# Value tiles padded by the host to full width, and value rows loaded one chunk ahead, in a chunked recurrence followed by a mixture of experts

## The chip, the core and the metric

One core of a Trainium2 chip runs the whole program. The metric is the time of one execution in device microseconds (us), the median of several runs. Engines are named as the profile names them: PE (TensorE), DVE (VectorE), ACT (ScalarE), POOL (GpSimd) and SP (SyncE, which here issues nearly all transfers).

## What is computed

The first stage is a recurrence over 768 time steps for 4 batches of 8 heads, with a 40x40 state per head. The second stage is a mixture of 8 experts over the 3072 x 320 result, with weights P from a gate that a Sinkhorn iteration balances.

```python
for t in range(S):
    y[:, :, t] = einsum('bhd,bhde->bhe', rt, state)
    Sa = einsum('bhde,bhe->bhd', state, at)
    state = state * wt[:, :, None, :] - einsum('bhd,bhe->bhde', Sa, bt) + einsum('bhd,bhe->bhde', vt, kt)
...
for e in range(E):
    out += P[:, e:e + 1] * (np.maximum(x @ w1[e], 0.0) @ w2[e])
```

All data are 32-bit floats. `v` holds the value rows of the recurrence (`vt` in the code above, one vector of 40 per head and step).

## The kernel before, in words

The recurrence is cut into 12 chunks of 64 steps (`C`, `NCH`). A unit of work is one chunk `c` of one batch `b`: eight heads, as four pairs (`NP`). The two heads of a pair stand on partitions 0 to 39 and 64 to 103 of tiles with 104 partitions (`R2`), and unused partitions hold zeros.

Work that doesn't depend on the state is done ahead by `prep(c, b)`. It loads one packed tile `inp` (L109, w, k, b and a of the unit), makes decay products by scans on DVE (`q` L114, `g` L122), the scaled `kb` and `ab` on DVE or POOL (L133, L139, L140), the products `ll` and the transposes `kt` on PE (L145, L153), and stores a part `lt` to DRAM as `ld`. For every two chunks, triangular matrices from `ld` are inverted on DVE (L170 to L182, tiles `un`, `lu`, `pr`). The inverse goes through DRAM (`ud`, `nd`) into `td` and `tt` (`tload`, `tmat`).

The sequential part is `recur(c, b)`, 48 units. It is a generator with five steps. The first step issues three loads on SP: the value rows into the left 64 columns of each pair's part of the tile `vz` (L238), `rb` (L240), and the transposed values into columns 64 to 103 of each head's part of the tile `f` (L242). Then PE makes `av` from `vz` and `rb` (L251), and DVE masks it into the left 64 columns of `f` (L252). The following steps are `xc` (L259), `pu` (L270, which needs `tt`), `c` and `ws` (L277, L279), the outputs `y` (L281, stored to DRAM as `xd` by L285) and the new state `z` (L292). At the end the transposed state is copied by ACT into columns 64 to 103 of the next `vz` (L299, L300). That `vz` is taken from five buffers (`vz_b`) in rotation. At the program's start all five are cleared once on DVE (`clear`, L85), since the loads leave a part of them unwritten. `f` has three buffers and `rb` two. A store `lp` of gate products is fed in between (L307, L312).

The units of the four batches are interleaved: step k of unit (c, b) has the due time 5c + k + 1.1b, the preps, inversions and loads have due times of their own, and the events are emitted sorted by them. Within each engine a scheduler then places the instructions by its own simulation of the program. An engine runs its list strictly in order, so a waiting instruction holds up everything behind it, on SP too. Transfers issued on SP tell of their landing through eight counters, `DMAHW0` to `DMAHW7`, used in turn.

The second stage reads `xd` back as `xs` (L508, L510), splits it and the expert weights `ws` (L473) into high and low parts, and multiplies on PE (`p` L545, `op` L610). It starts while the last recurrence units run.

Of the kernel before, what the change touches and what calls it, by code (L numbers as in the profile page):

```python
# [17 lines left out]
NB, NH, S, D = 4, 8, 768, 40  # L18
C = 64
NCH = S // C  # L20
NP = 4
R2 = 104
# [6 lines left out]
def attention(ctx, tc, d, xd, ps, pq, pt, gs, lg):  # L29
    nc = tc.nc  # L30
# [35 lines left out]
    lg_b = [const.tile([128, 4 * NP, 64], F32, name="lg")]  # L66
    ab_b = [pin.tile([R2, NP, 128], F32, name=f"ab{i}") for i in range(2)]
    g1_b = [pin.tile([R2, NP, 64], F32, name=f"g1{i}") for i in range(1)]
    vz_b = [const.tile([R2, NP, 104], F32, name=f"vz{i}") for i in range(5)]
    c1_b = [const.tile([R2, NP, 104], F32, name=f"c1{i}") for i in range(2)]  # L70
# [10 lines left out]
    def clear():  # L81
        nc.gpsimd.memset(unf, 0.0)
        nc.gpsimd.memset(unf[:, 0:1024:33], 1.0)
        for t in vz_b + c1_b + lg_b:
            nc.vector.memset(t, 0.0)  # L85
        for t in tt_b:
            nc.gpsimd.memset(t, 0.0)
# [11 lines left out]
    def rot(key, lst):  # L99
        i = state[key]  # L100
        state[key] = (i + 1) % len(lst)
        return lst[i]
# [132 lines left out]
    def recur(c, b):  # L235
        pp = preps[c, b]
        vz, zc = vz_cur[b], zp[b]
        nc.sync.dma_start(out=vz[:, :, 0:64], in_=d["v"][c, b])  # L238
        rb = io.tile([R2, NP, 128], F32, name="rb", bufs=NRB)
        nc.sync.dma_start(out=rb, in_=d["r"][c, b])  # L240
        f = wk.tile([R2, NP, 2, 104], F32, name="f", bufs=NFB)
        nc.sync.dma_start(out=f[0:64].rearrange("s p h x -> s (p h) x")[:, :, 64:104],  # L242
                          in_=d["vt"][c, b].rearrange("s (g x) -> s g x", x=40))
        if zc is None:
            nc.gpsimd.memset(f[64:104].rearrange("s p h x -> s (p h) x")[:, :, 64:104], 0.0)
        else:
# [3 lines left out]
        for p in range(NP):  # L250
            nc.tensor.matmul(av[:, p], lhsT=vz[:, p], rhs=rb[:, p], start=True, stop=True)  # L251
        nc.vector.tensor_tensor(  # L252
            out=f[:, :, :, 0:64], in0=av,
# [30 lines left out]
        for h in range(2):  # L284
            nc.sync.dma_start(  # L285
                out=xd[h * 160:h * 160 + 160].rearrange("(p e) t -> e p t", e=40)[:, :, tok:tok + 64],
                in_=y[h * 64:h * 64 + 40])
# [7 lines left out]
        zt = ps.tile([40, NP, 104], F32, name="zt", tag="ps")  # L295
        for p in range(NP):
            nc.tensor.transpose(zt[:, p], z[:, p], ident[0:R2, 0:R2])
        vz = rot("vz", vz_b)
        nc.scalar.copy(out=vz[0:40, :, 64:104], in_=zt[:, :, 0:40])  # L299
        nc.scalar.copy(out=vz[64:104, :, 64:104], in_=zt[:, :, 64:104])  # L300
        zp[b] = z
# [19 lines left out]

    gq, gcount = deque(), [0]
    vz_cur = [rot("vz", vz_b) for _ in range(NB)]
    preps, invs, tts = {}, {}, {}

    def start_seg(s):
# [9 lines left out]
    def load_lu(s, n):  # L336
        ld = invs[s][0]
        for cc in range(n):
            for blk in range(2):
                for h in range(2):  # L340
# [3 lines left out]
                        in_=ld[cc, r0:r0 + 32].rearrange("j b p h s -> (b p) j h s")[:, :, h, r0:r0 + 32])  # L344

    ev = [(T_CLEAR, clear, ())]
    gens = {}
    def step(c, b):
        if (c, b) not in gens:
            gens[c, b] = recur(c, b)  # L350
        next(gens[c, b], None)
# [6 lines left out]
    for c in range(NCH):  # L358
# [3 lines left out]
        t = 5 * c + 2 - T_LEAD  # L362
# [3 lines left out]
    for s, cs in enumerate(GROUPS):  # L366
# [3 lines left out]
        for i in range(n):  # L370
            cb = (cs[0] + i // NB, i % NB)
            j = cb[0] * NB + cb[1] - NSX
            t = 5 * (j // 4) + 3 + SKEW * (j % 4) + 0.01
            t = max(t, t0 + P0 + PD * i) if s else -20 + 0.01 * i
# [54 lines left out]
def body(ctx, tc, d, out):  # L429
# [12 lines left out]
    with ExitStack() as actx:  # L442
        ps, pq, pt = (actx.enter_context(tc.tile_pool(name=f"a_ps{i}", bufs=n, space=bass.MemoryType.PSUM))
                      for i, n in enumerate((PC, PQ, PT)))
        nc.sync.dma_start(out=gs, in_=d["gate"])
        attention(actx, tc, d, xd, ps, pq, pt, gs, lg)
        nc.gpsimd.memset(ones, 1.0)
        nc.sync.dma_start(out=ident, in_=d["cst"][:, 232:360])
# [290 lines left out]
def _layout(inputs):  # L739
    g = {k: np.asarray(v, dtype=np.float32) for k, v in inputs.items()}  # L740

    def split(a):
        return a.reshape(NB, NP, 2, NCH, C, D).transpose(3, 0, 2, 5, 1, 4)

    def packed(a, fill=0.0):
        x = split(a)
        o = np.full((NCH, NB, R2, NP, C), fill, np.float32)
        o[:, :, 0:40] = x[:, :, 0]
        o[:, :, 64:104] = x[:, :, 1]
        return o  # L750

    w = packed(g["w"], 1.0)
    wr = np.zeros((NCH, NB, R2, NP, 65), np.float32)
    wr[..., 1:] = w[..., ::-1]
    wf = np.zeros((NCH, NB, R2, NP, 64), np.float32)
    wf[..., 1:] = w[..., :-1]
    wcat = np.concatenate([wr.reshape(NCH, NB, R2, 260), wf.reshape(NCH, NB, R2, 256)], -1)
    kb = np.stack([packed(g["k"]), packed(g["b"])], axis=4)
    inp = np.concatenate([wcat, kb.reshape(NCH, NB, R2, 512), packed(g["a"]).reshape(NCH, NB, R2, 256)], -1)
    x = split(g["r"])  # L760
    rb = np.zeros((NCH, NB, R2, NP, 2, C), np.float32)
    rb[:, :, 0:40, :, 0] = x[:, :, 0]
    rb[:, :, 64:104, :, 1] = x[:, :, 1]
    vt = g["v"].reshape(NB, NH, NCH, C, D).transpose(2, 0, 3, 1, 4).reshape(NCH, NB, C, NH * D)
    rows = [(2 * p + h) * D + e for h in range(2) for p in range(NP) for e in range(D)]
    w1 = g["moe_w1"].reshape(E, DM, FP, 2, 128)[:, rows].reshape(E, 2, 160, FP, 2, 128)
    w1 = w1.transpose(0, 3, 4, 1, 2, 5)
    wp = np.zeros((E, FP, 2, 2, 2, 128, 128), np.float32)
    wp[:, :, :, :, 0] = w1[:, :, :, :, 0:128]
    for i in range(3):  # L770
        wp[:, :, :, :, 1, 32 * i:32 * i + 32] = w1[:, :, :, :, 128:160]
    wp = wp.transpose(0, 1, 5, 2, 3, 4, 6).reshape(E, FP, 128, 2, 2, 256)
    w2 = g["moe_w2"].reshape(E, FP, 2, 128, DM).transpose(0, 1, 3, 2, 4).reshape(E, FP, 128, 2 * DM)
    wts = np.concatenate([wp[..., 1, 0, :], w2, wp[..., 0, 0, :], wp[..., 0, 1, :], wp[..., 1, 1, :]], -1)
    wg = g["moe_w_gate"].reshape(NP, 2, D, E).transpose(1, 2, 0, 3)
    gate = np.zeros((R2, NP, E), np.float32)
    gate[0:40], gate[64:104] = wg[0], wg[1]
    cst = np.zeros((128, 660), np.float32)
    i = np.arange(64)
    up = (i[:, None] < i[None, :]).astype(np.float32)  # L780
    cst[0:64, 0:64] = up
    cst[0:64, 64:128] = up
    cst[64:128, 64:128] = 1.0
    cst[0:64, 128:192] = up
    cst[64:128, 128:192] = up
    cst[:, 192:232] = 1.0
    cst[:, 232:360] = np.eye(128)
    cst[64:104, 360:400] = np.eye(40)
    cst[:, 400::65] = 1.0
    arrays = dict(inp=inp, r=rb.reshape(NCH, NB, R2, NP, 128), v=packed(g["v"]),  # L790
                  vt=vt, wts=wts, gate=gate, cst=cst)
    return {k: np.ascontiguousarray(v) for k, v in arrays.items()}

# [16 lines left out]
```

## Time and profile before

| what | value |
|---|---|
| median of 3 runs | 1891.57 us (1887.94 to 1893.3) |
| the profiled execution's own time | 1888.5 us |
| its span on the core | 1886.7 us |
| PE busy over the span | 1768.5 us (94%) |
| DVE busy over the span | 1395.1 us (74%) |
| first `pu` (needs the first inverse) | about 119 us |
| last `av` of the recurrence | 547.66 us |
| PE busy from 680 to 1887 us | 1202.71 of 1207 us |

The profiled execution's own time is 3.1 us below the median of the runs and lies between their ends. The span is counted from the first instruction. Rows of the profile with a time at their start are instructions or merged groups, in us from the start of the span, followed by their duration; a bracket holds the engine's idle time before it and what ended that. "SPq" is SP issuing or waiting. In the rows on stretches, each engine's busy time stands in turn, then the granted clock of PE as a share of full speed, the share of busy time of the 16 DMA engines, and GB/s.

### The profile page before, as it was taken

To read this page: it belongs to the slowest core of one execution; us is meant where nothing else is said; L and a number is where in the kernel's file an instruction comes from. 1 tells how busy PE (TensorE), PEld (TensorE's weight loads), DVE (VectorE), ACT (ScalarE), POOL (GpSimd) and SP (SyncE) were. 2 spreads that over 40 slices of the span, in tenths; PEclk is the share of its full clock that TensorE was granted. 3 is DMA by queue.
4 is the path that set the end of the run, shared out by engine and by line. 5 is a ranking of instruction groups with operands and counts; after the bars stand their busy time and mean duration, and the time that the engine had idled before them with its cause. 6 is when DMAs were issued, how large, how long until landed. Compare 5 with 4: busy or idle time off the path is not lost.

```text
span 1886.7 us, 31821 instructions
## 1 busy us (share of the span) xinstructions
PE 1768.5 (94%) x12035; PEld 1731.1 (92%) x12035; DVE 1395.1 (74%) x2330; ACT 853.9 (45%) x1845; POOL 896.9 (48%) x845
## 2 busy tenths in 40 slices
PE   4478989889998999999999999999999999999999
PEld 4368878789888999999999999999999999999999
DVE  7766768686579877776867777886776767777676
ACT  6346566655553444343433434345343433434342
POOL 6636457562345355371835628004461826537170
PEclk9568889988889999999999999999999999999999
DMA  8567777855732011110201102111110201111011
GB/s 192 102 131 160 137 156 144 176 128 102 164 96 70 32 43 37 37 61 14 73 26 49 55 19 74 55 33 38 37 55 19 73 19 56 37 37 57 17 37 42
DMA packets 187838, 136.26 MB, mean 72 GB/s; under 512 B 155941, under 2 KB 165285, under 8 KB 187685
## 3 DMA queue, kind: packets, MB, share of 16 engines
q1 hardware_dynamic: 184485, 128.98, 27.6%
q10 hardware_dynamic: 3200, 5.25, 1.1%
q8 instruction: 95, 1.56, 0.3%
q14 instruction: 58, 0.48, 0.1%
HBM read 113.74 MB, written 20.45 MB: 71 GB/s over the span
## 4 chain that ended last, share of the span: by engine, by line
PE 76%; DVE 10%; DMA 6%; issue 3%; POOL 2%; ACT 2%; SPq 1%; DVEq 0%; POOLq 0%; ACTq 0%
PE op L610 35%; PE p L545 32%; DMA inp<-in_inp_dram 2%; PE xc L259 2%; DVE pr L179 2%; PE pu L270 1%; PE av L251 1%; PE c L277 1%; DVE q L114 1%; PE ll L145 1%; PE lp L307 1%; PE gp L226 1%; DMA nd<-pr 1%; POOL ab L140 1%; DVE g L122 1%
## 5 line engine op out<-in xcount | busy, mean ns | idle before, releaser
L545 PE MATMUL p<-xch,wh 128*128 128x384 f32 (+1 forms) x1792 | 605.3, 339 | 5.2 <-DVE cs L654 1.8
L566 ACT ACTIVATE hh<-sm 128x384 fp32r<-128x384 f32 x512 | 269.5, 527 | 726.3 <-DVE sm L563 726.3
L610 PE MATMUL op<-wh,hh 128*128 128x320 f32 x1536 | 477.3, 311 | 1.0 <-ACT hh L566 0.9
L610 PE MATMUL op<-wl,hh 128*128 128x320 f32 x1536 | 474.7, 310 | 0.0
L610 PE MATMUL op<-wh,hl 128*128 128x320 f32 x1536 | 468.0, 310 | 4.4 <-DVE hl L569 4.4
L491 POOL TENSOR_TENSOR wl<-ws,wh 128x640 fp32r<-128x640 f32 x60 | 103.1, 1719 | 608.4 <-ACT wh L489 608.1
L569 DVE SCALAR_TENSOR_TENSOR hl<-sm,hh 128x384 fp32r<-128x384 f32 x512 | 370.8, 757 | 2.8 <-ACT hh L566 2.3
L545 PEld LDWEIGHTS p<-xch,wh 128*128 128x128 f32 (+1 forms) x1792 | 337.9, 189 | 8.4 <-DVE u L563 2.7
L545 PE MATMUL p<-xcl,wh 128*128 128x384 f32 x896 | 303.1, 338 | 0.0
L545 PE MATMUL p<-xch,wl 128*128 128x384 f32 x896 | 302.3, 337 | 0.0
L610 PEld LDWEIGHTS op<-wh,hh 128*128 128x128 f32 x1536 | 290.6, 189 | 1.7 <-ACT hh L566 1.5
L610 PEld LDWEIGHTS op<-wh,hl 128*128 128x128 f32 x1536 | 287.1, 188 | 5.4 <-DVE hl L569 5.3
L610 PEld LDWEIGHTS op<-wl,hh 128*128 128x128 f32 x1536 | 291.4, 190 | 0.0
L563 DVE TENSOR_TENSOR sm<-p,u 128x384 f32<-128x384 f32 x384 | 232.6, 615 | 9.2 <-PE p L545 0.4
L545 PEld LDWEIGHTS p<-xcl,wh 128*128 128x128 f32 x896 | 169.0, 189 | 0.0
L545 PEld LDWEIGHTS p<-xch,wl 128*128 128x128 f32 x896 | 169.0, 189 | 0.0
L563 DVE TENSOR_TENSOR sm<-p,p 128x384 f32<-128x384 f32 x128 | 71.3, 557 | 130.1 <-PE p L545 76.2
L563 DVE TENSOR_TENSOR p<-p,p 128x384 f32<-128x384 f32 x128 | 71.1, 555 | 101.5 <-PE p L545 101.0
L563 DVE TENSOR_TENSOR u<-p,p 128x384 f32<-128x384 f32 x128 | 70.8, 553 | 59.4 <-PE p L545 58.1
L145 PE MATMUL ll<-ab,kb 104*128 104x128 f32 x336 | 61.3, 340 | 50.6 <-POOL ab L140 22.2
L499 POOL TENSOR_TENSOR wl<-ss,wh 128x512 fp32r<-128x512 f32 x60 | 90.7, 1512 | 32.1 <-ACT wh L496 28.0
L145 PEld LDWEIGHTS ll<-ab,kb 104*128 104x128 f32 x336 | 53.2, 241 | 54.7 <-POOL ab L140 27.4
(161 smaller groups left out, 2845.0 us busy)
## 6 DMA issues: line engine op xcount, KB each, us to landing
ws<-in_wts_dram SPq DMA_DIRECT2D x60, 832.0 KB
inp<-in_inp_dram SPq DMA_DIRECT2D x42, 521.6 KB
rb<-in_r_dram SPq DMA_DIRECT2D x48, 208.0 KB
ld<-lt ACTq DMA_DIRECT2D x40, 128.0 KB
vz<-in_v_dram SPq DMA_DIRECT2D x48, 104.0 KB
f<-in_vt_dram SPq DMA_DIRECT2D x48, 80.0 KB
xd<-y SPq DMA_DIRECT2D x96, 40.0 KB
st<-in_inp_dram SPq DMA_DIRECT2D x6, 521.6 KB
```

The source lines that it names most:

```text
L114: nc.vector.tensor_tensor_scan(out=q.rearrange("r p t -> r (p t)"), data0=w65[:, 0:260], data1=one65, initial=0.0, op0=ALU.mult, op1=ALU.add)
L122: nc.vector.tensor_tensor_scan(out=g.rearrange("r p t -> r (p t)"), data0=w65[:, 260:516], data1=g1.rearrange("r p t -> r (p t)"), initial ...
L145: nc.tensor.matmul(ll[:, p], lhsT=kb[:, p], rhs=ab[:, p], start=True, stop=True)
L179: nc.vector.tensor_tensor(out=prv, in0=a.unsqueeze(2).broadcast_to([nu, n_c, n_r, n_k]), in1=m.rearrange("u k r -> u r k").unsqueeze(1).br ...
L259: nc.tensor.matmul(xc[h][:, p], lhsT=pp["sx"][:, p, h], rhs=f[:, p, h], start=True, stop=True)
L491: g.tensor_tensor(out=wl[:, 0:640], in0=raw[:, 256:896], in1=wh[:, 0:640], op=ALU.subtract)
L499: g.tensor_tensor(out=lv[:, 3:7], in0=so[:, :, 0], in1=hv[:, 3:7, 0], op=ALU.subtract)
L545: nc.tensor.matmul(o, lhsT=w_, rhs=x_, start=(j == 0), stop=(j == 3))
L563: eng.tensor_tensor(out=out, in0=x, in1=y, op=ALU.add)
L566: nc.scalar.activation(out=hh[:, f, h], in_=sm[f][:, h], func=AF.Relu)
L569: v.scalar_tensor_tensor(out=hl[:, f, h], in0=sm[f][:, h], scalar=0.0, in1=hh[:, f, h], op0=ALU.max, op1=ALU.subtract)
L610: nc.tensor.matmul(ops[i], lhsT=a[:, h, cs], rhs=w_[:, cw], start=(f == 0 and h == 0 and j == 0), stop=(last and h == 1 and j == 2))
```

## The change

The host pads the value rows from 64 to 104 columns per pair (`vp`, zeros in columns 64 to 103) and the transposed values from 40 to 104 columns per head (`vq`, zeros in columns 0 to 63). The loads then write whole tiles, one contiguous piece for each partition: 104 pieces of 1664 bytes instead of 416 of 256 bytes for `vz`, and 64 pieces of 3328 bytes instead of 512 of 160 bytes for `f`. The zeros that the load puts into columns 0 to 63 of `f` are overwritten by DVE's mask, so L252 (L253 after the change) now writes after that load. The five clears of `vz` are dropped.

The value rows of unit (c + 1, b) are loaded by the first step of unit (c, b), into a buffer that is taken from the rotation there instead of at the unit's end. The four tiles of chunk 0 are loaded ahead of all events. The last chunk issues no value load; there are still 48 in all.

```diff
     def clear():
...
-        for t in vz_b + c1_b + lg_b:
+        for t in c1_b + lg_b:
             nc.vector.memset(t, 0.0)
...
     def recur(c, b):
         pp = preps[c, b]
         vz, zc = vz_cur[b], zp[b]
-        nc.sync.dma_start(out=vz[:, :, 0:64], in_=d["v"][c, b])
+        if c + 1 < NCH:
+            vn = rot("vz", vz_b)
+            nc.sync.dma_start(out=vn, in_=d["v"][c + 1, b])
         rb = io.tile([R2, NP, 128], F32, name="rb", bufs=NRB)
         nc.sync.dma_start(out=rb, in_=d["r"][c, b])
         f = wk.tile([R2, NP, 2, 104], F32, name="f", bufs=NFB)
-        nc.sync.dma_start(out=f[0:64].rearrange("s p h x -> s (p h) x")[:, :, 64:104],
-                          in_=d["vt"][c, b].rearrange("s (g x) -> s g x", x=40))
+        nc.sync.dma_start(out=f[0:64].rearrange("s p h x -> s (p h x)"), in_=d["vt"][c, b])
...
-        vz = rot("vz", vz_b)
+        vz = vn
         nc.scalar.copy(out=vz[0:40, :, 64:104], in_=zt[:, :, 0:40])
...
     vz_cur = [rot("vz", vz_b) for _ in range(NB)]
+    for b in range(NB):
+        nc.sync.dma_start(out=vz_cur[b], in_=d["v"][0, b])
...
-    arrays = dict(inp=inp, r=rb.reshape(NCH, NB, R2, NP, 128), v=packed(g["v"]),
+    vp = np.zeros((NCH, NB, R2, NP, 104), np.float32)
+    vp[..., 0:64] = packed(g["v"])
+    vq = np.zeros((NCH, NB, C, NH, 104), np.float32)
+    vq[..., 64:] = vt.reshape(NCH, NB, C, NH, D)
+    vt = vq.reshape(NCH, NB, C, NH * 104)
+    arrays = dict(inp=inp, r=rb.reshape(NCH, NB, R2, NP, 128), v=vp,
```

The order rows below come from the built programs. After the change L238 is L240, L240 is L242, L242 is L244 and L326 is the load of chunk 0. On SP, at the program's start, before and after:

```order
L40 DMA cst<-in_cst_dram 128x660
L109 DMA st_148<-in_inp_dram 104x1284
L109 DMA st_147<-in_inp_dram 104x1284
L109 DMA st_146<-in_inp_dram 104x1284
L109 DMA st_189<-in_inp_dram 104x1284
L109 DMA inp<-in_inp_dram 104x1284 x2
L238 DMA vz_197<-in_v_dram 104x4x64 [waits DMAHW0_49,DVE_49]
L240 DMA rb<-in_r_dram 104x512 [waits DMAHW1_49]
```

```order
L40 DMA cst<-in_cst_dram 128x660
L326 DMA vz_197<-in_v_dram 104x416
L326 DMA vz_198<-in_v_dram 104x416
L326 DMA vz_199<-in_v_dram 104x416
L326 DMA vz_200<-in_v_dram 104x416
L109 DMA st_148<-in_inp_dram 104x1284
L109 DMA st_147<-in_inp_dram 104x1284
L109 DMA st_146<-in_inp_dram 104x1284
L109 DMA st_189<-in_inp_dram 104x1284
L109 DMA inp<-in_inp_dram 104x1284 x2
L240 DMA vz_201<-in_v_dram 104x416
L242 DMA rb<-in_r_dram 104x512
```

Four value loads now stand ahead of the first six loads of `inp` (the first four of these go into tiles named `st`), and a fifth stands ahead of the first `rb`.

On DVE, after the fourth prep of the start (`f` is the mask of the first unit's `av`, `q` the scan of the fifth prep, `sx` a mask of the third), before and after:

```order
L139 TENSOR_TENSOR ab_195<-st_189,g_163 40x4x64
L140 TENSOR_TENSOR ab_195<-st_189,g_163 40x4x64
L252 TENSOR_TENSOR f<-av,cst 104x8x64
L114 SCALAR_TENSOR_TENSOR q<-inp,cst 104x260
L118 RECIPROCAL g_196<-q 104x4
```

```order
L139 TENSOR_TENSOR ab_195<-st_189,g_163 40x4x64
L140 TENSOR_TENSOR ab_195<-st_189,g_163 40x4x64
L114 SCALAR_TENSOR_TENSOR q<-inp,cst 104x260
L155 TENSOR_TENSOR sx_157<-ll,cst 64x8x64
L253 TENSOR_TENSOR f<-av,cst 104x8x64
L118 RECIPROCAL g_196<-q 104x4
```

The mask of the first `av` moved behind one scan and one mask of the preps.

On SP, in the recurrence, the loads of one unit with what each waits for (PE: a product that still reads the buffer), before and after:

```order
L285 DMA xd<-y 40x4x64 [waits DMAHW2_49]
L242 DMA f<-in_vt_dram 64x8x40 [waits DMAHW3_49,DVE_49,PE_49]
L240 DMA rb<-in_r_dram 104x512 [waits DMAHW4_49,PE_49]
L238 DMA vz_200<-in_v_dram 104x4x64 [waits DMAHW5_49]
L109 DMA inp<-in_inp_dram 104x1284 [waits DMAHW6_49,DVE_49,Pool_49]
```

```order
L286 DMA xd<-y 40x4x64 [waits DMAHW2_49]
L244 DMA f<-in_vt_dram 64x832 [waits DMAHW3_49,DVE_49,PE_49]
L240 DMA vz_200<-in_v_dram 104x416 [waits DMAHW4_49,PE_49]
L242 DMA rb<-in_r_dram 104x512 [waits DMAHW5_49]
L109 DMA inp<-in_inp_dram 104x1284 [waits DMAHW6_49,DVE_49,Pool_49]
```

The wait for PE moved from the load of `rb` to that of `vz`, which now stands ahead of it; the load of `vz` that stands beside one unit's `rb` belongs to the unit before.

On SP, where the second stage's first loads begin (`ws` are expert weights, `xs` the recurrence's output read back), before and after:

```order
L217 DMA tt_191<-ud 32x16x32
L238 DMA vz_197<-in_v_dram 104x4x64
L238 DMA vz_198<-in_v_dram 104x4x64
L473 DMA ws<-in_wts_dram 128x1664 x2
L242 DMA f<-in_vt_dram 64x8x40
L508 DMA xs<-xd 128x2x256
```

```order
L244 DMA f<-in_vt_dram 64x832
L217 DMA tt_191<-ud 32x16x32 x4
L476 DMA ws<-in_wts_dram 128x1664 x2
L511 DMA xs<-xd 128x2x256
L286 DMA xd<-y 40x4x64 x2
L513 DMA xs<-xd 32x2x256 x4
```

The value loads are gone from this place, and the loads of `xs` stand ahead of a load of `f` that was ahead of them.

## The prediction

> **What bounds the kernel now.** I read the table by stretches first. Its columns are the stretch, its length, the busy time of PE, of PE's weight loads, of DVE, ACT and POOL, then the granted clock, the DMA engines' busy share and GB/s:
>
> ```profile
> 0.00:40.00 40.00, 19.60 (x114) 18.07 (x115) 33.37 (x57) 25.00 (x60) 25.17 (x43) 0.98 0.86 206
> 280.00:320.00 40.00, 36.66 (x329) 34.15 (x327) 33.19 (x56) 24.29 (x62) 24.89 (x24) 0.91 0.68 136
> 480.00:520.00 40.00, 37.20 (x341) 35.11 (x342) 18.14 (x29) 23.48 (x55) 15.10 (x17) 0.83 0.77 174
> 680.00:1887.00 1207.00, 1202.71 (x7561) 1201.88 (x7559) 886.59 (x1512) 478.99 (x943) 547.92 (x473) 1.00 0.13 42
> ```
>
> From 680 us on PE is busy 1202.71 of 1207 us at full clock. That part holds nothing that the change touches, so only the first 560 us can move. The program's first 40 us are different: PE is half idle, DVE is busy 33.37 us, and the transfers run at 206 GB/s with 86% of the DMA engines' time taken. The timeline of that stretch shows who waits:
>
> ```profile
> 2.24 2.17 DVE L85 MEMSET vz<- 104x416 f32 x5
> 7.43 0.70 DVE L114 TENSOR_TENSOR_SCAN q<-st,cst 104x260 f32<-104x260 f32 x1 [1.06 <-DMA st<-in_inp_dram]
> ...
> 21.44 0.42 DVE L140 TENSOR_TENSOR ab<-st,g 40x256 f32<-40x256 f32 x1
> 24.08 0.69 DVE L252 TENSOR_TENSOR f<-av,cst 104x512 f32<-104x512 f32 x1 [2.22 <-PE av L251]
> 24.69 0.69 DVE L114 TENSOR_TENSOR_SCAN q<-inp,cst 104x260 f32<-104x260 f32 x1
> ...
> 28.24 0.68 DVE L155 TENSOR_TENSOR sx<-ll,cst 64x512 f32<-64x512 f32 x1
> ```
>
> ```profile
> 22.04 2.01 PE L251 MATMUL av<-rb,vz 104*104 104x128 f32 x8 [5.97 <-DMA rb<-in_r_dram]
> ```
>
> DVE begins at 7.43 us, when the first `inp` has landed, runs four preps without a pause, and then stands for 2.22 us at the mask of the first `av`. PE had waited 5.97 us for that `av`'s `rb`, which was queued behind six loads of `inp`. The chain of waits starts in the same way, and these are among its long pieces:
>
> ```profile
> 1.64 5.69 DMA st<-in_inp_dram
> ...
> 51.46 4.98 DMA lu<-ld
> ...
> 111.25 3.87 SPq L217
> 115.17 3.63 DMA tt<-ud
> ```
>
> Up to the first `tt`, about 119 us, the chain is one serial path (prep, `ld`, `lu`, inverse, `tt`), so a delay of DVE at the start delays everything. In the recurrence the question is whether anyone waits for `v` or `vt`. Here are the rows on the tile `vz` (durations are minimum, median and maximum in ns), two rows on the waits for it, then the rows on the other two loads:
>
> ```profile
> L238 SPq DMA_DIRECT2D vz<-in_v_dram x48: 824/868/5052, 4.6 to 504.4; - x48
>   DMA rb<-in_r_dram: 6.0, 1
>   PE zt L297: 5.0, 8
> ...
> L240 SPq DMA_DIRECT2D rb<-in_r_dram x48: 318/445/1557, 5.7 to 529.9; - x48
> ...
> L242 SPq DMA_DIRECT2D f<-in_vt_dram x48: 540/582/1832, 7.3 to 527.0; - x48
> ```
>
> The only wait of `av` for a transfer is the one at 22 us. The last value load is issued at 504.4 us, long before the last `av` (547.66 us, the chain's row):
>
> ```profile
> 547.66 1.05 PE av L251 x8
> ```
>
> With five buffers and the scheduler's order the rows are already early. In the recurrence it is `inp` that is waited for, and SP itself waits for its buffers (waits from 120 to 555 us; total, times, longest):
>
> ```profile
> DVE q L114 <- DMA inp<-in_inp_dram: 20.5, 15, 3.3
> ACT sx L141 <- DMA inp<-in_inp_dram: 4.7, 1, 4.7
> ...
> SPq L285 <- POOL y L281: 43.3, 26, 3.3
> SPq L242 <- PE xc L259: 29.5, 15, 3.7
> SPq L240 <- PE av L251: 6.6, 6, 2.3
> ```
>
> **The change part by part.**
>
> *Transfer time.* The sizes before come from the issue rows, the packets from the page:
>
> ```profile
> vz<-in_v_dram SPq DMA_DIRECT2D x48, 104.0 KB
> f<-in_vt_dram SPq DMA_DIRECT2D x48, 80.0 KB
> DMA packets 187838, 136.26 MB, mean 72 GB/s; under 512 B 155941, under 2 KB 165285, under 8 KB 187685
> q1 hardware_dynamic: 184485, 128.98, 27.6%
> q10 hardware_dynamic: 3200, 5.25, 1.1%
> q8 instruction: 95, 1.56, 0.3%
> q14 instruction: 58, 0.48, 0.1%
> ```
>
> I split the DMA engines' time into a price per byte and one per packet. From 680 us on, 13% of 16 engines' 1207 us is 2511 engine-us for 42 GB/s x 1207 us = 50.7 MB of large packets: 49.5 engine-us per MB. The whole span has about 29.1% (27.6, with 1.5 of the small queues) x 16 x 1886.7 = 8784 engine-us. Less 2511 that leaves 6273 for 85.6 MB, of which bytes take 4237. The other 2036, over some 180,000 packets, are an estimate of 11.3 ns a packet. The change removes 48 x (416 + 512) = 44,544 packets and adds 48 x (104 + 64) = 8,064: 36,480 fewer x 11.3 ns = 412 engine-us saved. It raises `v` to 169 KB and `vt` to 208 KB, 9.5 MB in all, x 49.5 = 470 engine-us added. The balance is +58 engine-us, 3.6 us of all 16 engines spread over 555 us. I take zero. [...]
>
> *Four value loads ahead of the first `inp`.* They are 4 x 169 KB = 0.69 MB, at the stretch's 206 GB/s 3.4 us. The bounds are 0 (they slip into time in which the queue stands empty) and 3.4; since DVE waits for exactly this transfer (the 1.06 us row), I take 3.4. [...] Against it, the mask of the first `av` now stands behind one scan and one mask (0.69 and 0.68 us, rows at 24.69 and 28.24), which fill part of the stall that moves along with `rb`: -1.4. Start: **+2.0 us**, between 0 and +3.5.
>
> *The clears.* 2.17 us of DVE go, at 2.24 us, ahead of a wait that ends with the transfer at 7.43. That transfer hides them: 0. If it came earlier, they would be worth 1 us.
>
> *SP's issue time.* A value load takes SP 868 ns with 416 pieces; `rb`, 104 pieces, takes 445. I give both new loads `rb`'s price: 48 x (0.42 + 0.14) = 27 us of SP. On the path lies only what stands directly ahead of a load that is waited for. In SP's list `inp` often follows `vz`. With 16 waits for `inp`, at most 16 x 0.56 = 9 us; at least 0, since SP mostly stands at a wait for a buffer and not at issuing. I take a quarter: **-2.3 us**.
>
> *The wait for the buffer.* The load of `vz` takes over the wait for an earlier `av` that `rb` had (6.6 us in 6 times). Both stand side by side, so what is queued behind (`inp`, the stores of `y`, the next `f`) waits for the same event: 0, if the two really come at the same time.
>
> *The mask after the load of `f`.* L253 now needs the landing of `f`, and behind it on DVE stand the preps and inversions. But SP issues `f` when the `xc` of three units earlier is done (29.5 us row), over ten us ahead of its mask: 0, if that lead holds.
>
> *The second stage's start.* Here the rows are these, SP's at the hand-over and the chain's:
>
> ```profile
> 498.44 1.80 SPq L238 DMA_DIRECT2D vz<-in_v_dram  x2
> 502.62 0.60 SPq L242 DMA_DIRECT2D f<-in_vt_dram  x1
> 503.26 0.61 SPq L508 DMA_DIRECT2D xs<-xd  x1
> ...
> 503.26 5.28 DMA xs<-xd
> 514.54 2.56 DMA xs<-xd
> 517.22 2.76 DVE xt L517
> ```
>
> SP works through a dense list here, and `xs` at 503.26 stands behind two value loads (1.80 us) and an `f` that waited for PE. The last `xs` of the first group comes at 514.54. After the change the value loads are gone from here, and the group stands ahead of `f`. It can come up to 9 us earlier (about 505 instead of 514.54), while DVE is busy only 18.14 of 40 us. But the recurrence units compete for DVE there, and PE is busy 37.20 of 40. Bounds -9 and +3 (one unit's masks and sums late behind the x work, by the row of 2.76 us); I take **-3 us**.
>
> *Order elsewhere.* The scheduler reshuffled PE's and DVE's lists from 120 us on. Nothing in the trace prices that. With PE 3 to 5 us idle in each 40, a per cent or so of the 435 us, 5 us either way, is my bound: 0.
>
> Sum: 2.0 - 2.3 - 3.0 = -3.3 us. The profiled execution's 1888.5 would become 1885.2. It lies 3.1 us below the median of the runs, so on the median I forecast 1891.6 - 3.3 = **1888.3 us**, -0.17%. A measurement of this kernel can tell about 0.3% (5.7 us) from no change, so this counts as no difference.
>
> **The rivals.**
>
> *Cheaper transfers (faster).* If small packets cost more than my estimate, for instance the mean packet's 8332 engine-us / 184485 = 45 ns, the change frees 36,480 x 45 ns / 16 = 103 us of DMA time and spends 29. Then `inp` lands earlier: half of its 25.2 us of waits gone is -12.6, with the start's +2.0 and the hand-over's -3 about -13.6 us: **1878 us**. For it: 155,941 of 187,838 packets are under 512 B, and transfers take 68% of the time in mid-recurrence. [...] Against it: 206 GB/s at 86%, with small packets among them, isn't far from the large packets' price.
>
> *SP blocked by the value load (slower).* The wait for `av` now stands ahead of `rb`, `inp` and the stores, with one unit's less lead. It decides once `av` is done later than the moment at which SP reaches the load. If the 6.6 us of L240's wait become as long as those of L242 (29.5 us) and half of the increase of 23 us passes through `inp` to DVE and PE, that is +11.5; with the start's +2.0, **1905 us**. Against it: the scheduler placed the load beside the `rb` of the next unit, where the same wait stood before.
>
> *Only the start counts.* The value rows were already early, so the prefetch changes nothing; the hand-over gains nothing since PE is nearly full: +2.0, **1893.6 us**.
>
> **How the numbers follow.** I give my forecast 0.40, cheaper transfers 0.32, SP blocked 0.16, only the start 0.12. Of the forecast's 0.40, 0.08 falls below the 0.3% bound by the unpriced order, and 0.02 above. So faster 0.32 + 0.08 = 0.40; slower 0.16 + 0.02 = 0.18; same 0.30 + 0.12 = 0.42. The range goes from 1875 (cheaper transfers, with some of the order's 5 us) to 1902 (most of the way to SP blocked).
>
> **What would show it.** Right: the first `q` on DVE at about 10.8 us; one short wait at the first mask; the value load on SP at about 0.45 us; waits for `inp` within a few us of 25; the first `xt` some us ahead of 517 relative to the last `av`. Wrong: SP's wait for `av` at the value load above 20 us (the slower rival); waits for `inp` halved and the DMA share in mid-recurrence well below 0.68 (the faster one); the last `av` moved by more than 10 us with none of these rows changed, which would leave the order.

## The result, and the profile after

| what | before | after |
|---|---|---|
| median on the same chip | 1889.76 us (1883.56 to 1893.3) | 1942.38 us (1941.05 to 1955.14) |
| ratio, 95% interval | | 1.0288 (1.0255 to 1.0321) |
| the profiled execution, its span | 1888.5 us, 1886.7 us | 1941.32 us, 1939.5 us |

The change makes the kernel 52.6 us slower. I had forecast 1888.3 us, no difference that can be measured, and my range ended at 1902.

The page of after first: busy times and, in 40 slices of the span, the granted clock.

```profile
PE 1814.9 (94%) x12035; PEld 1770.8 (91%) x12035; DVE 1394.6 (72%) x2325; ACT 854.3 (44%) x1845; POOL 902.2 (47%) x845
PEclk8568877987768999999999999999999999999999
```

The same lines of before:

```profile
PE 1768.5 (94%) x12035; PEld 1731.1 (92%) x12035; DVE 1395.1 (74%) x2330; ACT 853.9 (45%) x1845; POOL 896.9 (48%) x845
PEclk9568889988889999999999999999999999999999
```

PE runs the same 12035 matmuls and is busy for 46.4 us more. Its idle time grows little: 1886.7 - 1768.5 = 118.2 us before, 1939.5 - 1814.9 = 124.6 after. So the span grew mostly because PE took longer over the same work, at a lower granted clock (a mean of 0.921 over the span instead of 0.945), and not because it stood longer. The digits of the clock are lower in the first, the sixth and seventh and the tenth to thirteenth slice, and higher in none; a slice is 47 us before and 48 after.

The rows on the recurrence, from 120 us to the end of its last `av`, and on the second stage (columns as in the prediction), after:

```profile
120.00:595.42 475.42, 425.68 (x3422) 395.11 (x3422) 319.51 (x486) 262.77 (x653) 227.01 (x228) 0.79 0.66 147
720.00:1939.00 1219.00, 1215.11 (x7631) 1213.60 (x7630) 892.49 (x1523) 486.61 (x959) 557.76 (x481) 1.00 0.13 42
```

and the recurrence before:

```profile
120.00:548.71 428.71, 390.20 (x3438) 364.17 (x3437) 315.58 (x481) 262.85 (x653) 213.95 (x228) 0.87 0.67 143
```

For about the same matmuls PE is busy 35.5 us longer, at a mean clock of 0.79 instead of 0.87, and idle 11.2 us longer (49.7 us instead of 38.5). The second stage keeps its pace, at full clock. The last `av` of after:

```profile
594.07 1.35 PE L252 MATMUL av<-rb,vz 104*104 104x128 f32 x8
```

It ends at 595.42 us, where it ended at 547.66 + 1.05 = 548.71 before: 46.7 us of the 52.8 us by which the span grew are lost by then, 6.1 us behind it.

Now the steps at the program's start. The first scan `q`, the fifth, and the mask of the first `av` on DVE, and the first unit's `pu` on PE, after:

```profile
10.05 0.70 DVE L114 TENSOR_TENSOR_SCAN q<-st,cst 104x260 f32<-104x260 f32 x1 [5.88 <-DMA st<-in_inp_dram]
...
23.92 0.70 DVE L114 TENSOR_TENSOR_SCAN q<-inp,cst 104x260 f32<-104x260 f32 x1
...
27.26 0.69 DVE L253 TENSOR_TENSOR f<-av,cst 104x512 f32<-104x512 f32 x1 [2.07 <-PE av L252]
```

```profile
116.20 2.03 PE L271 MATMUL pu<-x,tt 128*128 128x104 f32 x8
```

and the first `pu` before, at 117.83 us (my table ahead of the prediction had about 119):

```profile
117.83 2.04 PE L270 MATMUL pu<-x,tt 128*128 128x104 f32 x8 [3.33 <-ACT tt L233]
```

The first `q` is 2.6 us late and the mask 3.2 us late. The fifth `q`, which now stands ahead of the mask, is 0.8 us early (24.69 before), and the first `pu` is 1.6 us early. So the delay of the start is gone before the first inverse.

Who waits in the recurrence (120 to 610 us), DVE and PE first, then SP:

```profile
DVE lg L313 <- PE lp L308: 39.3, 14, 9.0
DVE q L114 <- DMA inp<-in_inp_dram: 32.1, 12, 9.2
DVE pr L170 <- DMA lu<-ld: 16.9, 4, 7.3
PE gp L226 <- DMA td<-nd: 9.3, 4, 4.9
...
SPq L286 <- POOL y L282: 84.1, 24, 9.3
SPq L244 <- PE xc L260: 31.0, 11, 6.5
SPq L240 <- PE av L252: 13.3, 14, 3.4
```

Three of these rows before:

```profile
DVE lg L312 <- PE lp L307: 19.1, 13, 2.9
...
PE gp L226 <- DMA td<-nd: 4.0, 4, 1.5
...
DVE pr L170 <- DMA lu<-ld: 3.2, 1, 3.2
```

The value load on SP after:

```profile
L240 SPq DMA_DIRECT2D vz<-in_v_dram x44: 308/331/3732, 6.5 to 548.8; - x44
```

The loads that the change touches have no long wait: SP's wait for `av` at the value load is 13.3 us, and no row tells of anyone who waits for `vz` or `f` to land. What became long are waits inside the recurrence, the waits for `inp` (32.1 us, from 20.5) and those for the inverse. One place where much is lost at once is the end of the last inverse. There `gp` and `op` are PE's products that turn the loaded inverse `td` into `tt`, and `lp` is a product of the gate. DVE, SP, PE and POOL there, after:

```profile
524.91 1.30 DVE L334 COPY pr<-un 128x1024 f32<-128x1024 f32 x1
...
529.52 1.15 SPq L211 DMA_DIRECT2D td<-nd  x2
532.70 1.88 PE L226 MATMUL gp<-td,lg 64*64 64x32 f32 x16 [4.87 <-DMA td<-nd]
...
538.32 0.16 DVE L313 COPY lg<-lp 64x8 f32<-64x8 f32 x1 [9.04 <-PE lp L308]
538.36 0.73 POOL L282 TENSOR_TENSOR y<-ws,g 104x256 f32<-104x256 f32 x1 [13.07 <-PE lp L308]
```

and before:

```profile
483.75 1.29 DVE L331 COPY pr<-un 128x1024 f32<-128x1024 f32 x1
...
492.56 1.12 PE L226 MATMUL gp<-td,lg 64*64 64x32 f32 x16
```

Before, PE met `gp` when the inverse was there. After, it stands 4.87 us for it, everything behind it in PE's list stands too, and DVE (9.04) and POOL (13.07) stand for a PE product from behind `gp`. Four stretches around this place; the second has most of the stall, and the cuts lie 0.24 us behind the points at which the records let the clock change, hence 0.97:

```profile
516.54:526.78 10.24, 7.19 (x73) 6.83 (x72) 10.04 (x10) 5.52 (x13) 0.97 (x2) 1.00 0.40 101
526.78:530.20 3.42, 1.05 (x12) 0.88 (x9) 1.18 (x3) 1.55 (x6) 0.00 (x0) 0.97 0.92 236
530.20:571.16 40.96, 37.62 (x226) 34.63 (x227) 13.33 (x25) 17.12 (x37) 19.21 (x19) 0.50 0.68 174
571.16:594.00 22.84, 21.32 (x206) 18.68 (x205) 17.19 (x26) 15.70 (x37) 11.29 (x13) 1.00 0.50 136
```

In the second PE is busy only 1.05 of 3.42 us; then the clock is at half for 41 us, in which PE does 226 matmuls where the 22.84 us behind it hold 206. At the rate of the last stretch 226 would take 25 us. So I estimate that the 16 us that are left were lost with the clock, beside the stall's 5; the two stretches' matmuls aren't the same ones.

### The profile page after: what moved, and what is told of

The parts are those of the page before. It is cut to its first block, busy times and chain, and to the rows that moved or that the text cites. A ratio compares the mean times of both kernels' runs of the same rounds, so it can differ in the third digit from the quotient of the medians.

```text
span 1939.5 us, 31822 instructions
## 1 busy us (share of the span) xinstructions
PE 1814.9 (94%) x12035; PEld 1770.8 (91%) x12035; DVE 1394.6 (72%) x2325; ACT 854.3 (44%) x1845; POOL 902.2 (47%) x845
## 2 busy tenths in 40 slices
DMA packets 151358, 145.75 MB, mean 75 GB/s; under 512 B 111397, under 2 KB 125733, under 8 KB 151205
## 3 DMA queue, kind: packets, MB, share of 16 engines
q1 hardware_dynamic: 148005, 138.47, 27.9%
## 4 chain that ended last, share of the span: by engine, by line
PE 67%; DVE 5%; issue 3%; POOL 2%; DMA 1%; ACT 1%; SPq 1%; POOLq 0%; DVEq 0%; ACTq 0%
PE op L613 33%; PE p L548 30%; DVE hl L572 1%; PE xc L260 1%; PE lp L308 1%; DMA inp<-in_inp_dram 1%; DVE sm L566 1%; PE pu L271 1%; PE av L252 0%; PE c L278 0%; DMA nd<-pr 0%; POOL wl L494 0%; PE op L231 0%; DVE u L566 0%; PE gp L226 0%
## 5 line engine op out<-in xcount | busy, mean ns | idle before, releaser
L548 PEld LDWEIGHTS p<-xch,wh 128*128 128x128 f32 (+1 forms) x1792 | 338.3, 189 | 11.2 <-DVE sm L566 4.8
L145 PE MATMUL ll<-ab,kb 104*128 104x128 f32 x336 | 66.2, 360 | 53.8 <-POOL kb L133 25.8
L145 PEld LDWEIGHTS ll<-ab,kb 104*128 104x128 f32 x336 | 57.6, 259 | 58.5 <-POOL kb L133 30.9
```

The costliest lines, as they stand in the source:

```text
L145: nc.tensor.matmul(ll[:, p], lhsT=kb[:, p], rhs=ab[:, p], start=True, stop=True)
L548: nc.tensor.matmul(o, lhsT=w_, rhs=x_, start=(j == 0), stop=(j == 3))
```

## The experiments

*Theory A*: the rearranged lists of PE, DVE, ACT and POOL cost the time. *Theory B*: the padded and early loads cost it, by bytes and waits. *Theory C*: SP's rearranged list. To part them I held the engines in a chosen order. A table holds the order of one kernel as places in the program's text, and each instruction is tied behind the one ahead of it, without a semaphore:

```diff
+def pin(tc):
+    traced = list(tc.nc.cur_bb.bb.instructions)
+    for name, text in PLACES.items():
...
+        for a, b in zip(order[:-1], order[1:]):
+            tc.add_manual_dep(own[b], own[a].name, mybir.DependencyInfo(
+                mybir.DependencyClass.NoSync, mybir.DependencyReason.DATA), reason="order")
...
         body(tc, d, out)
+        pin(tc)
```

**1. Loads against order.** Four kernels: each set of loads in the other kernel's order, with SP left to the scheduler and with SP held too.

> The changed kernel's loads, with the instructions of PE, DVE, ACT and POOL held in the order of the kernel before; SP's list is left to the scheduler. Theory A (the loss of about 52 us comes from the rearranged lists of the four engines): 1885 to 1900 us, PE at half clock for about 110 us between 120 and 600 us. Theory B (the padded loads and their waits cost the time): 1930 us or more, in any order. Theory C (SP's list alone): between, depending on where SP's list falls.

> The kernel before, its loads and clears unchanged, with PE, DVE, ACT and POOL held in the order of the changed kernel; SP's list is left to the scheduler. Theory A: 1930 to 1950 us. Theory B: 1885 to 1900 us. Theory C: between.

> The kernel before with all five engines, SP too, held in the order of the changed kernel, each value load at the place of the load with the same number. Theory A: 1930 to 1950 us, as the run without SP. Theory B: 1885 to 1900 us. Theory C: 1930 to 1950 us here, but near 1890 us in the run without SP.

> The changed kernel's loads with all five engines in the order of the kernel before. In that order some value loads come late; the padded load must land before ACT writes the state into the tile, so ACT may wait here. Theories A and C: 1885 to 1905 us, with a few us more where ACT waits for a value load. Theory B: 1930 us or more.

| loads | order | SP held | median | ratio |
|---|---|---|---|---|
| changed | before | no | 1907.71 us | 1.0116 (1.0077 to 1.0156) |
| changed | before | yes | 1904.01 us | 1.0080 (1.0045 to 1.0116) |
| before | changed | no | 1928.27 us | 1.0217 (1.0167 to 1.0267) |
| before | changed | yes | 1932.81 us | 1.0231 (1.0189 to 1.0272) |

The order alone costs 2.2%, the loads alone 0.8 to 1.2%; 0.8 + 2.2 is near the whole 2.9. SP's list makes no difference that these intervals show. Theory A holds for the larger part, but not for all: the changed loads in before's order, with SP free, lie 8 us above its range, and the reverse lies 2 us below. B holds for a smaller part, and C falls. No run holds a kernel in its own order, so the holding itself isn't tested alone; the nearest is the run on the value rows in part 2, held on all five engines, whose interval ends at 1.0058. With before's loads in the changed order and SP held, the clock is lower:

```profile
core 0: 1935.6 us, clock 0.922
```

1935.6 x 0.922 = 1785 us, and before's 1886.7 x 0.945 = 1783: the same amount of full-clock time, and more time lost to a lower clock. With the changed loads in before's order (SP free),

```profile
core 0: 1903.7 us, clock 0.944
```

1903.7 x 0.944 = 1797: nearly the clock of before, with 137.0 us of PE idle instead of 118.2. But one trace is one execution, and the span and clock of every run are on record. The time lost to the clock, span x (1 - clock), averages 101.7 us over before's 13 runs here, 139.8 and 144.3 in the changed order (SP free and held), and 112.1 with the changed loads (SP free, and held). So the order's cost is nearly all clock, and of the loads' cost (the mean span grows by 21.7 and 15.5 us) about half to two thirds is clock too.

**2. Which load.** Still in before's order on all five engines: `f` alone padded, then the value rows alone with their edit. Since SP is held too, each value load is issued where before's load with the same number was (the first at 4.32 us, before at 4.62, behind the first six loads of `inp`), so this second run tests the padding and the dropped clears, and not the early loads. The diff of the first against before (with `vq` on the host) is the one hunk of the change (the second run has the hunks on `vz`, `vn` and `vp` and the dropped clears):

```diff
-        nc.sync.dma_start(out=f[0:64].rearrange("s p h x -> s (p h) x")[:, :, 64:104],
-                          in_=d["vt"][c, b].rearrange("s (g x) -> s g x", x=40))
+        nc.sync.dma_start(out=f[0:64].rearrange("s p h x -> s (p h x)"), in_=d["vt"][c, b])
```

> Only the transposed values are padded (the load of f writes whole rows, the mask of av overwrites its zeros); the value rows are loaded as before; all five engines are held in the order of before. The changed loads as a whole had cost 10 to 19 us in before's order (1904 to 1908 against 1888.3). Theory F (the padding of f carries it: 2.6 times the bytes of vt, and DVE's mask now waits for the load): 1900 to 1908. Theory V (the value loads carry it): 1886 to 1892, no different from before.

> Only the value rows are padded and loaded a chunk ahead; f is loaded as before; all five engines are held in the order of before. Theory V (the value loads carry the 10 to 19 us, by 1.6 times the bytes or by four loads ahead of the first inp): 1900 to 1908. Theory F: 1886 to 1892. If both parts cost about half of it, each comes out near 1896.

`f` alone: 1900.32 us, 1.0073 (1.0044 to 1.0102). The value rows alone: 1890.96 us, 1.0027 (0.9996 to 1.0058). Theory F: the larger part of the loads' cost is the padding of `f`. Its trace shows where it begins. SP's first load of `lu`, which waits for the preps' stores, with `f` padded:

```profile
42.17 1.40 SPq L344 DMA_DIRECT2D lu<-ld  x3
```

and before:

```profile
38.77 1.40 SPq L342 DMA_DIRECT2D lu<-ld  x3
```

Each padded `f` is 208 KB instead of 80, and the first three stand between the loads of `inp` in the first 40 us, in which the DMA engines are busy 86% of the time before the change. The first `pu` comes at 122.93 us instead of 117.83, and the waits for `inp` later on are 34.8 us instead of 20.5.

To test that, the four `f` of chunk 0 went back to 160-byte pieces:

```diff
+        if c == 0:
+            nc.sync.dma_start(out=f[0:64].rearrange("s p h x -> s (p h) x")[:, :, 64:104],
+                              in_=d["vt"][c, b].rearrange("s (g x) -> s g x", x=104)[:, :, 64:104])
+        else:
+            nc.sync.dma_start(out=f[0:64].rearrange("s p h x -> s (p h x)"), in_=d["vt"][c, b])
```

> As the run with the padded f alone in before's order (1900.3, +0.73%), but the four f of chunk 0 are loaded as before, in pieces of 160 bytes; from chunk 1 on f is padded. Theory S (the padded f costs because its bytes stand ahead of the loads of inp at the program's start, where the transfers are full: the second unit's pu came 4.2 us later there and about 10 us at mid-recurrence): 1890 to 1895, with the loads of lu issued near 39 us as in before. Theory R (its cost is spread over the recurrence, by bytes or by the mask's wait): 1897 to 1903.

1898.19 us, 1.0045 (1.0016 to 1.0074); `lu` at 40.16, the first `pu` at 120.28. About half of the delay at the start is gone. The time lies in the range of theory R (spread over the recurrence) and above that of theory S (the start), but the interval overlaps that of `f` padded throughout, so a gain isn't shown. How much of `f`'s cost is the start and how much is spread stays open.

**3. Each part in its own order.** The same two, with the scheduler free:

> Only the transposed values are padded, and the scheduler orders the lists as it likes: 970 of PE's and 368 of DVE's instructions stand elsewhere than before, from the 599th of PE on, though nothing moves at the program's start. Theory A (a rearranged list costs time, whatever it was that moved it, since before's list is a lucky one): 1910 to 1935, with PE's clock from 120 to 600 us below 0.85. Theory A2 (it is the early value loads that make a bad list; padding f alone makes a harmless one): 1886 to 1900.

> Only the value rows are padded and loaded ahead, and the scheduler orders the lists as it likes: 876 of PE's and 329 of DVE's instructions stand elsewhere than before, from the 17th of PE on. Theory A: 1910 to 1935, as for the padding of f alone. Theory A2: near the whole change's 1930 to 1942, while the padding of f alone stays near 1890.

`f` alone: 1911.9 us, 1.0126 (1.0092 to 1.016). Value rows alone: 1909.09 us, 1.0104 (1.0064 to 1.0143). Both parts lead to a list that costs some 0.5 to 0.8% over the same loads in before's order (for `f` the two intervals still touch; for the value rows the loads are also early now). That is what theory A expected in kind (1910 to 1935), at its lower end and 1 us below it; A2, which spared `f`, falls.

**4. Lists redrawn by other edits.** Before with one constant changed, the changed kernel with the lead of the inverse's products half a step more or less, then with the first constant:

```diff
-L_LEAD = 0.5
+L_LEAD = 1.0
...
-T_LEAD = 2
+T_LEAD = 2.5
```

> The kernel before with all its loads as they were; one constant is changed (L_LEAD 0.5 to 1.0), so that the load of the inverse is handed to the scheduler half a step earlier. By itself that is a load issued a little earlier, worth nothing; but the scheduler answers by placing some 680 of PE's and 260 of DVE's instructions elsewhere. Theory A (before's list is a chosen one among many, and nearly any other costs 0.5% or more): 1896 to 1925. Theory A2 (only the changed loads lead to a bad list): 1882 to 1892.

> The changed kernel with the constant T_LEAD 2.5 in place of 2: loads and products of the inverse (td, gp, op, tt) are handed to the scheduler half a step earlier. Theory I (the changed list loses because the inverse comes late at the segments' ends, and PE stands at gp for td): PE meets gp still earlier and waits longer, 1940 to 1965. Theory A (each list is a draw): anywhere from 1900 to 1950, without relation to td.

> The changed kernel with T_LEAD 1.5: products of the inverse are handed to the scheduler half a step later, nearer to their use in pu. Theory I: PE no longer stands at gp for td; 1905 to 1925, and PE's wait for td is gone from the table of waits. Theory A: anywhere from 1900 to 1950, without relation to td.

> The changed kernel with L_LEAD 1.0 in place of 0.5, the constant that made before's list 0.58% slower. Theory A (each list is a draw; the changed loads cost 0.8% by themselves, and lists cost 0.5 to 2.8%): 1905 to 1955, with no preference. Theory A3 (the changed loads bring about a list that is bad in a particular way, so that all lists of the changed kernel are): 1930 to 1955, as for the three lists of it so far (1942, 1934, 1957).

| kernel | median | ratio |
|---|---|---|
| before, `L_LEAD` 1.0 | 1900.09 us | 1.0058 (1.0024 to 1.0092) |
| changed, `T_LEAD` 2.5 | 1934.19 us | 1.0278 (1.0223 to 1.0333) |
| changed, `T_LEAD` 1.5 | 1957.11 us | 1.0356 (1.0306 to 1.0405) |
| changed, `L_LEAD` 1.0 | 1919.48 us | 1.0174 (1.0132 to 1.0216) |

I take the first row's edit, a load issued a little earlier, to have no weight in itself; then its list costs 0.6%. Theory I (PE meets `gp` too early) falls with the second and third: the earlier lead was to lose, and came out no worse than the change itself; the later lead was to gain, and lost, and PE still waits 7.3 us for `td` there. The third also lies 7 us above the range that theory A gave (1900 to 1950). The fourth lies below the range that A3 gave for every list of the changed kernel.

One more list comes from the value rows loaded ahead without any padding:

```diff
-        nc.sync.dma_start(out=vz[:, :, 0:64], in_=d["v"][c, b])
+        if c + 1 < NCH:
+            vn = rot("vz", vz_b)
+            nc.sync.dma_start(out=vn[:, :, 0:64], in_=d["v"][c + 1, b])
...
+    for b in range(NB):
+        nc.sync.dma_start(out=vz_cur[b][:, :, 0:64], in_=d["v"][0, b])
```

> The kernel before with nothing padded and the clears kept; only the value rows are loaded one chunk ahead, in the scheduler's own order (785 of PE's instructions elsewhere). Nothing waits for the value rows in before, and their bytes and pieces are the same, so the loads themselves are worth 0, or the start's few us. Theory A: the rearranged list costs 0.5% or more, 1896 to 1925. Theory A3: it is the padding that leads to bad lists; 1885 to 1893.

1914.48 us, 1.0145 (1.0098 to 1.0191). In this version the clears stand behind the loads of chunk 0 and overwrite its value rows with zeros, so it computes something else with the same instructions. Its first scan comes 3.4 us late (10.80 us), since the first load of `inp` is issued 3.7 us later, behind four value loads; 3.3 us of that are left at the third unit's `av`. The rest of the 26 us is in line with A: no padding is needed for a bad list.

**5. Where in the list.** Before's loads, with the changed order up to the 22nd unit and before's behind it, and the reverse (held as in part 1, with a table of places joined from the two):

> The kernel before with its own loads; PE, DVE, ACT and POOL are held in the changed kernel's order up to the 22nd unit (about 335 us) and in before's order from there on. The whole of the changed order had cost 1.0217 (41 us), of which 17 us had come up by the 23rd unit's av and 45 us by the 45th. Theory P (spread: a few us at each segment of the inverse): 1903 to 1910. Theory Q (the loss sits at the last segment and the hand-over to the second stage): 1888 to 1894.

> The reverse: before's order up to the 22nd unit, the changed order from there on, loads of before. Theory P: 1903 to 1915, so that the two halves together make the 41 us. Theory Q: 1922 to 1930, all of it.

First half: 1899.4 us, 1.0059 (1.0028 to 1.0091). Second half: 1922.05 us, 1.0168 (1.0114 to 1.0222). Neither theory came out: the first time lies between the ranges of P (spread) and Q (all at the end), and the second at the lower end of Q's. Together the halves make the 2.2%, a quarter of it in the first and three quarters in the half that has the late last inverse. In the second run PE and DVE stand there as in after:

```profile
511.82 1.89 PE L229 MATMUL gp<-td,lg 64*64 64x32 f32 x16 [3.85 <-DMA td<-nd]
517.44 0.16 DVE L315 COPY lg<-lp 64x8 f32<-64x8 f32 x1 [8.38 <-PE lp L310]
```

Last, I exchanged nothing but the places of the 134 inversion steps on DVE between the two lists (again by the table):

> Loads of before; PE, DVE, ACT and POOL in the changed kernel's order (1.0217), but on DVE the steps of the inversions after the start (134 instructions) stand between the recurrence's masks and sums where before's list has them. Theory I (the inversions' place on DVE makes the steps at the segments' ends): 1.004 to 1.012, PE's wait at gp for td gone. Theory J (their place is a victim, the loss lies in how PE, POOL and DVE interleave the recurrence's steps): 1.017 to 1.025.

> The reverse: loads of before and order of before, only these 134 steps on DVE stand where the changed list has them (SP is left to the scheduler). Theory I: 1.010 to 1.018. Theory J: 0.998 to 1.006.

In the changed order with before's places: 1935.26 us, 1.0229 (1.0195 to 1.0263), no gain, and PE's wait for `td` is still 7.2 us (before 4.0). In before's order with the changed places: 1919.94 us, 1.0154 (1.0129 to 1.0179). The answers disagree: the changed places alone are enough to lose 1.5%, but undoing them repairs nothing. So the late inverse is one place where the loss comes up, not its single cause. My reading, which no run isolates, is that a list works as a whole: steps of one engine that fit the other engines' lists don't fit another's.

None of the 19 programs beats the kernel before.

## Why the prediction was wrong, step by step

- **What bounds the kernel.** Right that only the first 560 us can move: the second stage kept its pace. Wrong in what I read from it. I took PE's busy time as given and looked for changes of its idle time.
- **Order elsewhere: 0, with 5 us either way.** This is the step that failed, and it is nearly the whole miss. I bounded it by PE's idle time in each 40 us. Measured, the order costs 2.2% (1.0217 and 1.0231), about 41 to 44 us, while PE's idle time grew by only 7 to 9 us (125.6 and 127.6 against 118.2). Most of the loss lies in PE's busy time. The row for the bound was on the page: a granted clock of 0.83 to 0.91 in the recurrence, so that the same matmuls could take longer. I quoted it and gave it no term. My last signpost, the last `av` moved by more than 10 us with none of the loads' rows changed, fits in part: it moved by 46.7 us and the signs of both rivals stayed away, though the waits for `inp` had grown.
- **Transfer time: 0.** Wrong by about 14 us, the 0.73% of the padded `f`. The balance of bytes and packets was off as well. The row of the loads' queue, after and with `f` alone padded:

```profile
q1 hardware_dynamic: 148005, 138.47, 27.9%
```

```profile
q1 hardware_dynamic: 162981, 135.28, 28.8%
```

  27.9% of 1939.5 us is 541 us of each of the 16 engines, and 28.8% of 1897.7 us is 547; before, 27.6% of 1886.7 us was 521. So the transfers took 20 us more where I had 3.6, and with `f` alone 26. The bytes that the padding of `f` adds (6.3 MB) would take 19.5 us at my price, so the packets that it saves show no gain at all. And I spread the cost over 555 us, but the bytes of `f` also fall into the first 40 us, ahead of loads of `inp` that DVE waits for, which I priced for the value rows alone.
- **Four value loads ahead of `inp`: +2.0 us.** The first `q` came 2.6 us late (I had 3.4), but by the fifth nothing was left of it, and the first `pu` came 1.6 us early, in another order. What the early loads cost in one order stays open: in before's order with SP free, where they do stand ahead of `inp`, the first `pu` comes at 124.16 us, and with SP held, where they don't, at 120.68, but the two times (1.0116 and 1.0080) can't be told apart.
- **The clears: 0.** As said: DVE idles 5.88 us ahead of the first `q`.
- **SP's issue time: -2.3 us.** The value load fell to 331 ns, below the 445 that I took, and no gain followed: the waits for `inp` went up, from 20.5 to 32.1 us, and with the padded value rows alone in before's order nothing was won (1.0027). No run shows SP's issue time on the path.
- **The wait for the buffer, and the mask behind the load of `f`: 0 each.** Nothing in the rows speaks against it: 13.3 us in 14 waits, 3.4 at most, and no wait for `f`'s landing. The slower rival, SP blocked by the value load, needed 29.5 us and did not happen: the kernel is slower by another way.
- **The second stage's start: -3 us.** The first `xt` did move ahead, to 46.4 us before the last `av` from 30.4:

```profile
547.68 0.42 DVE L520 TENSOR_TENSOR xt<-xs 128x256 f32<-128x256 f32 x1 [2.43 <-DMA xs<-xd]
```

  but the time behind the last `av` grew by 6.1 us. By the clock records 23.9 us are at half clock there, against 10.2 before, and half of the difference is 6.8 us; why the clock is lower there no run shows.
- **Cheaper transfers (rival).** 111397 packets under 512 B are left of 155941, and the DMA engines' share did not fall (27.9% for the queue above, from 27.6). The trace shows no gain from removing 44,544 of them, at the price of 9.5 MB more, and no run shows that a small packet costs more than my 11.3 ns; this rival's 45 ns was the mean packet's time, taken as an estimate.

What stays open: why the changed loads together lead to lists that cost more than those of either part. The four lists of the changed kernel cost 1.7 to 3.6%, the others 0.6 to 1.5% in full; with so few draws I can't say whether the loads bring this about or chance does.

## What to carry to other kernels

Where a scheduler fills in-order queues, an edit to a few loads redraws every list, and that redraw can have a price of its own: here 0.5 to 2.2%, and for the whole change more than the 0.8 to 1.2% of its loads. Price it, or hold the old order and measure the edit alone. And where the granted clock of the bounding engine is below 1, its busy time is not a constant (here 1768.5 and 1814.9 us for the same 12035 matmuls): bound a new stall by the clock that it may cost, not by its own length.

## What the runs showed of the hardware

All twenty programs do the same PE work (12035 matmuls, before as after), and the spans of their profiled executions differ by up to 70 us (1885.3 to 1955.8). Yet span times mean granted clock is 1783 to 1799 us in each of these executions (before 1783, after 1786, the slowest 1955.8 x 0.916 = 1792). One and the same program moves in this way too: ten runs of the changed loads in before's order, SP held, go from 1887.5 us at a clock of 0.950 to 1915.7 at 0.930, which is 1793 and 1782.

Short stalls often go ahead of a drop. By the clock records, each of the two traces has 15 drops to half clock between about 120 us and the last `av`. In the 3.41 us ahead of them PE was busy 1.00 to 2.17 us in 9 cases of before and 1.08 to 2.32 us in 12 of after, and 2.58 to 3.42 us in the others. The half-clock stretch lasts 3.41 to 17.07 us before and 3.41 to 40.96 us after. Two places in after, the stretch with the stall and the one behind it, besides that at 530 us (cut 0.24 us late as above):

```profile
444.87:448.28 3.41, 1.68 (x23) 1.48 (x21) 0.68 (x1) 1.92 (x6) 0.05 (x1) 0.97 0.80 136
448.28:468.76 20.48, 18.30 (x114) 17.52 (x115) 5.11 (x9) 7.93 (x22) 4.29 (x6) 0.51 0.77 152
...
496.07:499.48 3.41, 1.99 (x25) 1.74 (x23) 3.41 (x4) 1.00 (x3) 2.34 (x2) 0.97 0.12 27
499.48:516.54 17.06, 16.30 (x97) 15.46 (x97) 10.16 (x13) 6.86 (x18) 2.82 (x2) 0.51 0.35 84
```

and one in before:

```profile
413.81:417.22 3.41, 1.46 (x16) 1.49 (x17) 3.35 (x7) 0.47 (x1) 2.98 (x4) 1.00 0.54 137
417.22:420.63 3.41, 3.41 (x21) 3.31 (x20) 3.41 (x6) 3.25 (x9) 0.67 (x2) 0.50 0.46 90
```

PE was busy 1.46 to 1.99 of the 3.41 us, and half clock followed. It lasted 3.41 us in one case, with PE busy all the time, and 17 to 41 us in others (that at 530 us among them) in which PE was busy 89 to 96% of the time. The busy time of the 3.41 us ahead alone doesn't decide it. Here the clock stayed full behind 3.42 us in which PE was busy 1.80 us (after):

```profile
519.72:523.14 3.42, 1.80 (x19) 1.83 (x20) 3.42 (x4) 1.22 (x4) 0.00 (x0) 1.00 0.65 184
523.14:526.55 3.41, 2.69 (x28) 2.47 (x26) 3.41 (x6) 2.08 (x5) 0.73 (x1) 1.00 0.41 85
```

and here it fell behind 3.42 us in which PE was busy throughout (before):

```profile
444.52:447.94 3.42, 3.42 (x38) 3.02 (x38) 2.50 (x10) 2.63 (x7) 0.78 (x2) 1.00 0.78 160
447.94:451.35 3.41, 3.41 (x19) 3.29 (x20) 2.48 (x5) 1.30 (x4) 0.00 (x0) 0.50 0.64 106
```

In the last 17 us of the stretch at 530 us PE doesn't stand at all, and the clock stays at half:

```profile
553.86:570.92 17.06, 17.06 (x102) 15.66 (x102) 8.56 (x13) 10.79 (x22) 14.75 (x13) 0.50 0.45 125
```

The 15 stretches of each trace are all whole multiples of 3.41 us in length; they add up to 109 us before and 201 after. Half of the difference is 46 us, about the 46.7 us by which the last `av` came later. So between these two it is not more drops, it is longer ones. What ends a stretch I did not find, and that the clock is the cause and not a companion of the loss was read from the traces and the runs' clocks, not tested by an edit that keeps PE busy in the stalls.
